# Output rows of a mixture-of-experts kernel: plain stores in token order in place of indexed writes

## The chip, the cores and the metric

The kernel runs on one core of one Trainium2 chip. The metric is the device time of one execution in microseconds (us), the median over runs. TensorE (PE), VectorE (DVE), ScalarE (ACT), GpSimd (POOL) and SyncE (SP) are separate engines; each works through its own queue of instructions in the order in which they were written, and semaphores hold an instruction until what it needs is done. SP computes nothing: here it starts most of the transfers between memory and the on-chip buffers. POOL also starts transfers, those that take their row numbers from a table.

## The reference

Eight sequences, each with 512 tokens of width 512 and 32 state tokens. An attention step lets tokens read from the states and states read from the tokens; the 544 rows that result, per sequence, go through a mixture of eight experts with one expert per row:

```python
xread = softmax(x @ state.T / 8) @ state          # 512 rows a sequence
sread = softmax(state @ x.T / 8) @ x              # 32 rows a sequence
for b in range(B):
    prev_e = -1
    for s in range(S):                            # S = 544
        fresh_e = argmax(logits[b, s])
        e = fresh_e if s == 0 or local_gate[b, s] < 0.5 or prev_e < 0 else prev_e
        prev_e = e
        p = softmax(logits[b, s])
        out[b, s] = p[e] * (relu(x[b, s] @ w1[e]) @ w2[e])
```

A row may keep the expert of the row before it. With the data of this case all 512 tokens of a sequence end up with the expert of its first token; the kernel does not rely on that, it counts what is left over.

## The kernel before

**The work.** A *unit* is the 512 tokens of one sequence, done with the expert of its first token (`slots.units`). There are eight units. The two matrix products of a unit (512 x 512 x 1024 and 512 x 1024 x 512) use a seven-product scheme in place of eight block products: sums of blocks of weights and inputs are made first on DVE (`first_sum`, `second_sum`, `column_sum`), then `seven` runs products 1, 5, 6, 2, 7, 3, 4 on PE, and ACT and DVE combine the results. A unit has two first halves (`first_half(0)`, `first_half(1)`) and two second halves (`second_half(n)`), 28 products in all, some 1.73 us each. The state tokens of all sequences are sorted by expert into nine *tiles* of 32 rows by 4 quarter rows (`Tile`), which are placed between the halves of units 4 to 7. A general path (`rows_again`, `more`) under `tc.If(left > 0)` does the tokens whose expert isn't that of their unit. Here none are left, so every engine reads `left` (L1244), jumps over that code (L1246) and meets the others in the closing steps (L1281).

**The order.** It is written out by hand. After each product `seven` calls `tick()`, and work that belongs beside the products is registered by tick number: attention of sequences 2 to 7 (`FLOW`, 14 ticks a sequence), the sums, and the steps of the routing (`GROUPS`, seven ticks for each group of sequences, the steps of the generator `choose`). Steps registered for the same tick are issued in the order in which they were registered, attention ahead of routing. The second step of `choose` is one ACT instruction, `activation(pr, pr, Act.Exp)` at L582. It needs `pr`, which the first step makes with its last DVE instruction (L579). For the first group of sequences these two steps are at ticks 6 and 7; tick 7 is the last of `first_half(0)` of unit 0, so that the exponent stands on ACT just ahead of the copy of product 1 of `first_half(1)` into `sum` (L995, `nc.scalar.copy(y, x)`). Product 6 adds to `sum`, so PE needs that copy.

**The output.** `second_half(n)` makes two blocks of 128 rows: `y0`, complete after product 3 (L1113), and `y1`, complete after product 4 (L1117 or L1119). Each is written with an indirect transfer from POOL (`scatter`, L1038): the row numbers are in `slots.tok`, made by one DVE instruction in `choose` (L615) from a table of token numbers (`self.token`, two POOL instructions in `more_constants`) and with 8192 added for a token that is not done here, so that the bounds check drops its row. The write of `y0` is issued at once; that of `y1` goes into the list `behind` and is issued during the next half. A tile's result is put into the same list and is written, also indirectly, by `Tile.scatter` (L985). The write of a unit's rows is declared free of dependencies only where `apart` is set, that is in the last `second_half` of the last unit (`scatter(..., not late)`). The others, and all writes of tiles, may touch any row of `out` as far as the framework can tell, so each waits until the one before it has landed. In that last half (`seven(..., apart=True)`) the list `waiting` holds the `y1` of the half before and the result of the last tile: the first is issued after product 6, the second after product 7.

**SP's queue.** SP starts the loads of weights (`load`, L842), of the units' inputs (`load_x`, L845), of the tiles' weights (L952, L954), of the attention's inputs (L292, L296), and the attention's stores (L463, L418). A load into a buffer waits on SP until the buffer's last reader is done, and everything behind it on SP waits too. Each of these transfers also waits until the one eight places earlier on SP has landed, since they share eight semaphores in turn. `load(u + 1, 1)`, the second weights of the next unit, comes right after the last `second_half` of unit `u`.

Of the kernel before, what the change touches and what calls it, by code (L numbers as in the profile page):

```python
# [18 lines left out]
P = 128  # L19
# [3 lines left out]
T = S + N  # L23
# [93 lines left out]
class Slots:  # L117


    def __init__(self, pool):  # L120

        self.tok = pool.tile([P, B, SC], I32, name="tok")
        self.prob = pool.tile([P, B, NC], F32, name="prob")
        self.state = pool.tile([P, NTILE], I32, name="state")
        self.row = pool.tile([P, NTILE], I32, name="row")
        self.probq = pool.tile([P, NTILE], F32, name="probq")
        self.rest_tok = pool.tile([P, NB], I32, name="rest_tok")
        self.rest_row = pool.tile([P, NB * Q], I32, name="rest_row")
        self.rest_prob = pool.tile([P, NB], F32, name="rest_prob")
        self.first = pool.tile([1, 1], I32, name="first")  # L130
        self.units = pool.tile([1, B], I32, name="units")
        self.tiles = pool.tile([1, NTILE], I32, name="tiles")
        self.rest = pool.tile([1, NREST], I32, name="rest")
        self.left = pool.tile([1, 1], I32, name="left")
        self.number = pool.tile([1, 1], I32, name="number")
# [23 lines left out]
"""  # L159
FIRST, PERIOD = 2, 14  # L160
PER = 28
GROUPS = {(0, 2): (6, 7, 10, 11, 13, 14, 15), (2, 4): (55, 56, 57, 59, 61, 62, 63),
          (4, 8): (102, 103, 105, 106, 109, 110, 111)}
ONES = 18, 19, 21, 22, 24, 25, 27, 28, 29

# [304 lines left out]
class Routing:  # L470
# [16 lines left out]
    def more_constants(self):  # L487
        nc, rt = self.nc, self.rt
        pi = rt.tile([P, 1], I32, name="pi")
        nc.gpsimd.iota(pi, pattern=[[0, 1]], base=0, channel_multiplier=1)  # L490
        ti, ci, bi = [rt.tile([P, B, NC], I32, name=n) for n in ("ti", "ci", "bi")]
        nc.gpsimd.iota(ti, pattern=[[T, B], [P, NC]], base=0, channel_multiplier=1)
        nc.gpsimd.iota(ci, pattern=[[-T // LOW, B], [-P // LOW, NC]], base=NT // LOW, channel_multiplier=0)
        nc.gpsimd.iota(bi, pattern=[[-1, B], [0, NC]], base=B, channel_multiplier=0)
        self.iob = rt.tile([P, P], BF16, name="iob")
        nc.gpsimd.tensor_copy(self.iob, self.io)
        self.identb = rt.tile([P, P], BF16, name="identb")
        nc.gpsimd.tensor_copy(self.identb, self.ident)
        self.part = rt.tile([P, 1], F32, name="part")
        nc.gpsimd.tensor_copy(self.part, pi)  # L500
        self.token = rt.tile([P, B, NC], F32, name="token")
        nc.gpsimd.tensor_copy(self.token, ti)
        self.ones = rt.tile([P, P], BF16, name="ones")
        nc.gpsimd.memset(self.ones, 1.0)
        self.one = rt.tile([1, P], F32, name="one")
        nc.gpsimd.memset(self.one, 1.0)
        self.on = rt.tile([P, E, COLS + 1], F32, name="on")
        nc.gpsimd.memset(self.on, 1.0)
        nc.gpsimd.memset(self.on[:, :, 0:1], 0.0)
        self.ons = rt.tile([SQ, E, B + 1], F32, name="ons")  # L510
        nc.gpsimd.memset(self.ons, 1.0)
        nc.gpsimd.memset(self.ons[:, :, 0:1], 0.0)
        self.turn = rt.tile([P, Q, SQ], BF16, name="turn")
        nc.gpsimd.tensor_copy(self.turn, self.iob[:, :SQ].rearrange("p (o t) -> p o t", o=1).to_broadcast([P, Q, SQ]))
        self.ex = rt.tile([P, B, NC], F32, name="ex")
        nc.gpsimd.memset(self.ex, 0.0)
        self.undone = rt.tile([P, B, NC], F32, name="undone")
        nc.gpsimd.memset(self.undone, 0.0)
        self.factors = rt.tile([P, B, NC, 6], BF16, name="factors")
        nc.gpsimd.tensor_copy(self.factors[:, :, :, 0], ci)  # L520
        nc.gpsimd.tensor_copy(self.factors[:, :, :, 5], bi)
        self.ev = rt.tile([P, E, 1], F32, name="ev")
        nc.vector.tensor_scalar(self.ev.rearrange("p e o -> p (e o)"), self.iof[:, :E], 1.0, None, Alu.add)
        self.before = rt.tile([P, P], BF16, name="before")
        nc.vector.tensor_scalar(self.before, self.iob, self.part, None, Alu.is_gt)
        nc.vector.tensor_scalar(self.factors[:, :, :, 1], self.ex, self.part, None, Alu.add)
        quarter = rt.tile([P, 1], I32, name="quarter_of")
        nc.vector.tensor_scalar(quarter, pi, SQ.bit_length() - 1, None, Alu.logical_shift_right)
        self.quarter = rt.tile([P, 1], F32, name="quarter")
        nc.vector.tensor_scalar(self.quarter, quarter, float(Q * NT), None, Alu.add)  # L530
        self.squarter = rt.tile([P, 1], F32, name="squarter")
        nc.vector.tensor_scalar(self.squarter, quarter, float(Q * B * N), None, Alu.add)
        self.mx = rt.tile([P, B, NC, 1], F32, name="mx")
        self.eq = rt.tile([P, B, NC, E], F32, name="eq")
        self.own = rt.tile([P, B, NC], F32, name="own")
        self.top = rt.tile([P, B, NC], BF16, name="top")
        self.pr = rt.tile([P, B, NC, E], F32, name="pr")
        self.zp = rt.tile([P, B, NC], F32, name="zp")
        self.oh = rt.tile([P, E, B, NC], BF16, name="oh")
        self.hold = rt.tile([B, T], BF16, name="hold")  # L540
        self.ran = rt.tile([B, T], BF16, name="ran")
        self.states = rt.tile([SQ, E, B], BF16, name="states")
# [13 lines left out]
    def choose(self, bank, b0, b1):  # L556
# [45 lines left out]
        for i in range(SC):  # L602
# [9 lines left out]
        nc.vector.scalar_tensor_tensor(self.undone[:, b, :SC], ex[:, b, :SC], -1.0,  # L612
                                       held.rearrange("p (b o) -> p b o", o=1).to_broadcast([P, n, SC]),
                                       Alu.add, Alu.not_equal)
        nc.vector.scalar_tensor_tensor(slots.tok[:, b], self.undone[:, b, :SC], float(OFF), self.token[:, b, :SC],  # L615
                                       Alu.mult, Alu.add)
        yield

        oh = self.oh[:, :, b].rearrange("p e b i -> p e (b i)")
# [188 lines left out]
class Experts:  # L808
# [84 lines left out]
    def run(self, start):  # L893
# [38 lines left out]
        class Tile:  # L932
# [49 lines left out]

            def scatter(self, y):
                at = bass.IndirectOffsetOnAxis(ap=slots.row[:, self.i:self.i + 1], axis=0)
                nc.gpsimd.indirect_dma_start(out=out.rearrange("n (q x) -> (n q) x", q=Q), out_offset=at, in_=y,  # L985
                                             in_offset=None, bounds_check=NT * Q - 1, oob_is_err=False)

        def seven(y, n, product, copies, whole, tick, waiting=(), apart=False):

# [9 lines left out]
            tick()  # L999
            product(y, 6)  # L1000
            two(y)
            for results in waiting[:1]:
                results()
            tick()
            product(x, 2)
# [2 lines left out]
            if apart:  # L1008
# [2 lines left out]
                tick()  # L1011
                product(y, 7)
                three(y)
                for results in waiting[1:]:
                    results()
                whole(4, None)
                tick()
                z = bank()[:, :n]
# [14 lines left out]
            whole(3, y)  # L1033
            tick()

        def scatter(at, y, apart=False):
            to = bass.IndirectOffsetOnAxis(ap=at, axis=0)
            put = nc.gpsimd.indirect_dma_start(out=out, out_offset=to, in_=y, in_offset=None, bounds_check=NT - 1,  # L1038
                                               oob_is_err=False)
            if apart:  # L1040
                tc.declare_no_dep(put.ins, group="scatters", reason="a token has one slot, so scatters write other rows")
                tc.add_to_no_dep_group("scatters", put.ins)

        def first_product(to, i, n, begin=False):

# [39 lines left out]
            seven(sums, 512, lambda to, i, begin=False: first_product(to, i, n, begin),  # L1085
                  [kept(flat(t)) for t in (s5, s2, s7)], whole, tick, waiting)

        def second_half(at, prob, n, tick, waiting, behind, late):
            ((d11, d12), (d21, d22)), wcs = places(1)
            seconds = {1: (h11, d11), 2: (h21, d21), 3: (hs[2], d22), 4: (h22, wcs[2]), 5: (hs[0], wcs[0]),  # L1090
                       6: (hs[1], wcs[1]), 7: (c12, d12)}
            r5, r2, r7 = [h1.tile([P, 2, UNIT // 2], F32, name=f"s{i}")[:, 0] for i in range(3)]
            at = [at[:, 2 * b + n:2 * b + n + 1] for b in range(2)]
            p0, p1 = [prob[:, 2 * b + n:2 * b + n + 1] for b in range(2)]
            y0, y1 = ys[2 * n:2 * n + 2]
            low, high = slice(0, D // 2), slice(D // 2, D)
# [10 lines left out]
            def second_whole(i, t):  # L1107
# [3 lines left out]
                    add(y1[:, high], r7, r5)  # L1111
                elif i == 2:
                    nc.vector.scalar_tensor_tensor(y0[:, high], t, p0, r2, Alu.mult, Alu.add)  # L1113
                    scatter(at[0], y0, not late)
                else:
                    if late:
                        scaled(y1[:, low], p1)(t)  # L1117
                    else:
                        nc.vector.scalar_tensor_tensor(y1[:, low], t, p1, r7, Alu.mult, Alu.add)  # L1119
                    behind.append(lambda: scatter(at[1], y1, not late))  # L1120

            seven(sums, D // 2, second, [scaled(r5, p1), scaled(r2, p0), scaled(r7, p1)], second_whole,
                  tick, waiting, apart=not late)
# [20 lines left out]
        def unit(u, waiting=()):  # L1144
# [9 lines left out]
                self.load_x(u + 1)  # L1154
                load(u + 1, 0)
            behind = []
            second_half(slots.tok[:, u], slots.prob[:, u], 0, self.tick, waiting, behind, True)
            bound(U * u + 2, behind)
            if not ahead:
                nc.gpsimd.drain()  # L1160
            waiting, behind = behind, []
            second_half(slots.tok[:, u], slots.prob[:, u], 1, self.tick, waiting, behind, ahead)
            bound(U * u + 3, behind)
            if not ahead:
                for results in behind:
# [51 lines left out]
        def more(v):  # L1217
# [15 lines left out]
                first_half(n, nothing)  # L1233
            for n in range(2):
                behind = []
                second_half(slots.rest_tok[:, U * v:U * v + U], slots.rest_prob[:, U * v:U * v + U], n, nothing, (),
                            behind, False)
                for results in behind:
                    results()
            if v + 1 < NREST:  # L1240
# [44 lines left out]
```

## Time and profile before

| what | value |
|---|---|
| median of 3 runs | 512.46 us (511.43, 512.46, 514.82) |
| the profiled execution's own time | 511.91 us |
| its span, first to last instruction | 510.1 us |
[...]
| busy, PE / DVE / ACT / POOL | 97% / 55% / 32% / 22% |
| DMA, mean rate | 227 GB/s |

The span is 1.8 us shorter than the execution's time; the rest lies around it. The median of the runs is 0.55 us above the profiled execution. An engine's busy share says how much of the span it had an instruction in work, whatever stage that was; the waits and the timeline say where an engine stood still and for whom.

### The profile page before, as it was taken

The numbers are of one execution on the slowest core, as the hardware profiler recorded it, in microseconds if no ns is written. First come the engines' busy times: TensorE is split into PE (matmuls) and PEld (weight loads), VectorE is DVE, ScalarE is ACT, GpSimd is POOL, SyncE is SP. The second block draws the span as 40 slices with busy tenths as digits, with TensorE's granted clock in tenths as the row PEclk, the third lists the DMA queues.
The fourth block names the chain that finished last, engine by engine and source line by source line (L and its number), as shares of the span: only waits on it lengthen the run. The fifth ranks groups of instructions, "written<-read, shape, count | busy, mean of one in ns | idle before, by whom it ended". The sixth has DMA issues, their size and how long they took to land. (4 is left out here: it accounts for less than half of the span.)

```text
span 510.1 us, 10091 instructions
## 1 busy us (share of the span) xinstructions
PE 494.8 (97%) x4008; PEld 390.4 (77%) x4008; DVE 282.0 (55%) x543; ACT 161.0 (32%) x334; POOL 111.6 (22%) x134
## 2 busy tenths in 40 slices
PE   8899999999999999999999999999999999999992
PEld 2457787776877778787888888888888888878881
DVE  5878885497765986436576745155342624346100
ACT  2625424353343443434223322223122321223210
POOL 6602232322232223220021202210101300121012
PEclk9999999999999999999999999999999999999997
DMA  8995472917649074441746976793989579593411
GB/s 306 348 331 185 163 278 108 358 35 258 243 135 340 26 261 159 141 175 55 275 129 223 400 249 213 246 410 128 397 330 350 202 279 410 194 340 125 169 41 53
DMA packets 38289, 115.67 MB, mean 227 GB/s; under 512 B 7749, under 2 KB 7881, under 8 KB 34009
## 3 DMA queue, kind: packets, MB, share of 16 engines
q1 hardware_dynamic: 34952, 105.37, 57.0%
q0 software_dynamic: 3136, 9.51, 4.9%
q8 instruction: 33, 0.54, 0.4%
q14 instruction: 24, 0.19, 0.1%
q10 hardware_dynamic: 144, 0.07, 0.0%
HBM read 97.10 MB, written 17.89 MB: 225 GB/s over the span
## 5 line engine op out<-in xcount | busy, mean ns | idle before, releaser
L1054 PE MATMUL ps<-x,a 128*128 128x256 f32 x384 | 92.8, 384 | 0.0
L1054 PE MATMUL sum<-xs,a 128*128 128x256 f32 x384 | 91.6, 381 | 1.2 <-ACT sum L995 1.2
L1038 POOL DMA_INDIRECT out_dram<-y,tok x32 | 37.2, 1163 | 236.3 <-DVE xs L852 47.8
L1054 PEld LDWEIGHTS sum<-xs,a 128*128 128x128 f32 x384 | 71.9, 190 | 15.9 <-issue 2.5
L1054 PEld LDWEIGHTS ps<-x,a 128*128 128x128 f32 x384 | 71.3, 190 | 14.5 <-issue 5.2
L1101 PE MATMUL ps<-c,h 128*128 128x256 f32 x264 | 63.8, 385 | 0.0
L1101 PE MATMUL ps<-c,hs 128*128 128x256 f32 x256 | 60.8, 380 | 0.0
L1101 PE MATMUL sum<-c,h 128*128 128x256 f32 x248 | 58.7, 379 | 0.0
L1101 PEld LDWEIGHTS ps<-c,h 128*128 128x128 f32 x264 | 49.0, 190 | 9.5 <-issue 2.9
L1101 PEld LDWEIGHTS ps<-c,hs 128*128 128x128 f32 x256 | 48.4, 190 | 9.0 <-issue 2.5
L1101 PEld LDWEIGHTS sum<-c,h 128*128 128x128 f32 x248 | 46.6, 190 | 6.1
L852 DVE TENSOR_TENSOR a<-a,a 128x1024 f32<-128x1024 f32 x32 | 40.2, 1294 | 4.5 <-DMA a<-in_w_dram 4.3
L852 DVE TENSOR_TENSOR c<-c,c 128x1024 f32<-128x1024 f32 x32 | 39.9, 1280 | 2.8 <-DMA c<-in_w_dram 2.5
L852 DVE TENSOR_TENSOR h<-s,s 128x512 f32<-128x512 f32 x16 | 11.1, 696 | 43.2 <-ACT s L1083 43.1
L995 ACT COPY sum<-ps 128x512 f32<-128x512 f32 (+1 forms) x32 | 14.8, 464 | 55.4 <-PE ps L1101 27.9
L1054 PE MATMUL ps<-xs,a 128*128 128x256 f32 x128 | 30.7, 382 | 0.5 <-DVE a L852 0.5
L1083 ACT COPY s<-sum 128x512 f32<-128x512 f32 x32 | 18.7, 585 | 38.5 <-PE sum L1054 30.3
L1101 PE MATMUL sum<-c,hs 128*128 128x256 f32 x128 | 30.9, 384 | 0.0
L1101 PEld LDWEIGHTS sum<-c,hs 128*128 128x128 f32 x128 | 23.8, 190 | 8.0 <-issue 2.5
L1105 ACT ACTIVATE s<-sum,prob 128x256 f32<-128x256 f32 x32 | 15.1, 473 | 46.1 <-PE sum L1101 44.9
L852 DVE TENSOR_TENSOR y<-s,s 128x256 f32<-128x256 f32 x16 | 6.8, 424 | 39.0 <-ACT s L1105 39.0
L1054 PEld LDWEIGHTS ps<-xs,a 128*128 128x128 f32 x128 | 24.0, 190 | 4.7 <-DVE a L852 1.4
(186 smaller groups left out, 562.9 us busy)
## 6 DMA issues: line engine op xcount, KB each, us to landing
at<-in_w_dram SPq DMA_DIRECT2D x18, 1024.0 KB, 7.4
ct<-in_w_dram SPq DMA_DIRECT2D x18, 1024.0 KB, 10.2
a<-in_w_dram SPq DMA_DIRECT2D x32, 512.0 KB, 7.8
c<-in_w_dram SPq DMA_DIRECT2D x32, 512.0 KB, 6.5
x_t<-in_xt_dram SPq DMA_DIRECT2D x16, 512.0 KB, 6.1
x_n<-in_xn_dram SPq DMA_DIRECT2D x8, 1024.0 KB, 6.9
xts<-xr SPq DMA_DIRECT2D x28, 256.0 KB, 2.1
x<-xts SPq DMA_DIRECT2D x7, 1024.0 KB, 5.8
```

The lines of the kernel that those rows point to most:

```text
L852: self.nc.vector.tensor_tensor(out, a, b, op=op)
L995: nc.scalar.copy(y, x)
L1038: put = nc.gpsimd.indirect_dma_start(out=out, out_offset=to, in_=y, in_offset=None, bounds_check=NT - 1, oob_is_err=False)
L1054: nc.tensor.matmul(to[:, m * width:m * width + width], lhsT=w[:, j, f:f + P], rhs=x[:, j, :], start=begin and m == 0 and j == 0, stop=(m = ...
L1083: return lambda t: nc.scalar.copy(to, t)
L1101: nc.tensor.matmul(to, lhsT=x[:, m, n * P:n * P + P], rhs=w[:, m, :], start=begin and m == 0, stop=(m == FK // 2 - 1), skip_group_check=True)
L1105: return lambda t: nc.scalar.activation(to, t, Act.Copy, scale=p)
```

## The change

- The rows of a unit are written by `unit_rows`, a plain store issued on SP, 128 consecutive rows of `out` each, at the same places in the order in which `scatter` stood. All rows are written, also those of tokens of another expert; the general path writes over them afterwards (`rest_rows`, the indirect write as before, ordered behind everything).
- The stores of units and the writes of tiles are declared to touch different rows, each towards the group of the other (`apart`). The writes of tiles stay in order among themselves.
- `slots.tok`, the table `token` and the instructions that make them are gone: two POOL instructions at the start, one DVE instruction in each of the three groups of `choose`.
- In the last half of the last unit everything in `waiting`, the last tile's write too, is issued after product 6.
- In the first group of sequences the exponent of `choose` moves from tick 7 to tick 9.

```diff
-GROUPS = {(0, 2): (6, 7, 10, 11, 13, 14, 15), (2, 4): (55, 56, 57, 59, 61, 62, 63),
+GROUPS = {(0, 2): (6, 9, 10, 11, 13, 14, 15), (2, 4): (55, 56, 57, 59, 61, 62, 63),
...
-        nc.gpsimd.iota(ti, pattern=[[T, B], [P, NC]], base=0, channel_multiplier=1)
...
-        self.token = rt.tile([P, B, NC], F32, name="token")
-        nc.gpsimd.tensor_copy(self.token, ti)
...
-        nc.vector.scalar_tensor_tensor(slots.tok[:, b], self.undone[:, b, :SC], float(OFF), self.token[:, b, :SC],
-                                       Alu.mult, Alu.add)
...
             def scatter(self, y):
...
+                put = nc.gpsimd.indirect_dma_start(out=out.rearrange("n (q x) -> (n q) x", q=Q), out_offset=at, in_=y,
+                                                   in_offset=None, bounds_check=NT * Q - 1, oob_is_err=False)
+                apart(put, "states", "x")
...
-            for results in waiting[:1]:
+            for results in waiting if apart else waiting[:1]:
                 results()
...
                 three(y)
-                for results in waiting[1:]:
-                    results()
...
+        def apart(put, rows, others):
+
+            tc.declare_no_dep(put.ins, group=others, reason="x tokens and state tokens have rows of their own")
+            tc.add_to_no_dep_group(rows, put.ins)
+
+        def unit_rows(u, c, y):
+            apart(nc.sync.dma_start(out=out[u * T + c * P:u * T + c * P + P], in_=y), "x", "states")
+
+        def rest_rows(v, c, y):
+            to = bass.IndirectOffsetOnAxis(ap=slots.rest_tok[:, U * v + c:U * v + c + 1], axis=0)
+            nc.gpsimd.indirect_dma_start(out=out, out_offset=to, in_=y, in_offset=None, bounds_check=NT - 1,
+                                         oob_is_err=False)
...
                     nc.vector.scalar_tensor_tensor(y0[:, high], t, p0, r2, Alu.mult, Alu.add)
-                    scatter(at[0], y0, not late)
+                    put(v, n, y0)
...
-                    behind.append(lambda: scatter(at[1], y1, not late))
+                    behind.append(lambda: put(v, 2 + n, y1))
...
-            second_half(slots.tok[:, u], slots.prob[:, u], 0, self.tick, waiting, behind, True)
+            second_half(unit_rows, u, slots.prob[:, u], 0, self.tick, waiting, behind, True)
...
-            second_half(slots.tok[:, u], slots.prob[:, u], 1, self.tick, waiting, behind, ahead)
+            second_half(unit_rows, u, slots.prob[:, u], 1, self.tick, waiting, behind, ahead)
```

## Rows read from the trace of the kernel before

**Rows 1.** Part 1 of the page: busy time, share of the span, instructions
```profile
PE 494.8 (97%) x4008; PEld 390.4 (77%) x4008; DVE 282.0 (55%) x543; ACT 161.0 (32%) x334; POOL 111.6 (22%) x134
```

**Rows 2.** PE's waits, first and last of eight: us in total, times, longest
```profile
PE sum L1054 <- ACT sum L995: 1.2, 1, 1.2
...
PE s L320 <- DMA x_t<-in_xt_dram: 0.2, 1, 0.2
```

**Rows 3.** Timeline of PE, 33 to 62 us: start us, us, engine, line, instruction, idle before
```profile
44.96 1.89 PE L1054 MATMUL ps<-xs,a 128*128 128x256 f32 x8
48.09 1.99 PE L1054 MATMUL sum<-xs,a 128*128 128x256 f32 x8 [1.24 <-ACT sum L995]
...
59.10 1.89 PE L1101 MATMUL ps<-c,h 128*128 128x256 f32 x8
60.83 1.46 PE L1101 MATMUL ps<-c,hs 128*128 128x256 f32 x6
```

**Rows 4.** Timeline of ACT, 40 to 66 us
```profile
47.28 0.27 ACT L582 ACTIVATE pr<-pr 128x80 f32<-128x80 f32 x1 [3.25 <-DVE pr L579]
47.45 0.58 ACT L995 COPY sum<-ps 128x512 f32<-128x512 f32 x1
```

**Rows 5.** Timeline of DVE, 33 to 62 us
```profile
47.01 0.23 DVE L579 TENSOR_TENSOR pr<-lt,mx 128x80 f32<-128x80 f32 x1
...
55.24 0.77 DVE L852 TENSOR_TENSOR h<-s,s 128x512 f32<-128x512 f32 x1 [0.36 <-ACT s L1083]
```

**Rows 6.** Timeline of all engines, 478 to 512 us
```profile
487.71 0.35 DVE L980 TENSOR_SCALAR yt<-ps,probq 128x128 f32<-128x128 f32 x1 [3.16 <-PE ps L976]
...
497.85 0.98 POOL L1038 DMA_INDIRECT out_dram<-y,tok  x1 [5.86 <-DVE y L1113]
...
499.97 0.48 DVE L1119 SCALAR_TENSOR_TENSOR y<-ps,prob,s 128x256 f32<-128x256 f32 x1 [0.80 <-PE ps L1101]
501.21 0.98 POOL L985 DMA_INDIRECT out_dram<-yt,row  x1 [2.39 <-DMA out_dram<-y,tok]
504.53 0.98 POOL L1038 DMA_INDIRECT out_dram<-y,tok  x1 [2.35 <-issue]
```

**Rows 7.** Line L1244, by engine: instruction, count, ns min/median/max, first and last start
```profile
L1244 SPq TENSOR_LOAD <-left x1: 275/275/275, 472.2 to 472.2; - x1
```

**Rows 8.** Line L1246, the jump over the general path, SP and ACT
```profile
L1246 SPq EVENT_SEMAPHORE  x9: 17/17/17, 478.2 to 478.8; - x9
...
L1246 ACTq EVENT_SEMAPHORE  x2: 17/17/17, 502.0 to 502.1; - x2
...
L1246 SPq COMPARE_BRANCH  x1: 45/45/45, 472.5 to 472.5; - x1
...
L1246 ACTq COMPARE_BRANCH  x1: 50/50/50, 498.8 to 498.8; - x1
```

**Rows 9.** Line L1281, the closing steps on SP
```profile
L1281 SPq EVENT_SEMAPHORE  x14: 17/28/28, 508.5 to 510.1; - x14
```

**Rows 10.** Line L463, stores of 256 KB from SP; us from issue to landing
```profile
L463 SPq DMA_DIRECT2D xts<-xr x28: 319/320/794, 34.0 to 241.5; - x28
...
DMA to landing us min/median/max: 2.0/2.9/6.9
```

**Rows 11.** Timeline of SP, 250 to 300 us: second weights of unit 4
```profile
258.63 9.76 SPq L842 DMA_DIRECT2D c<-in_w_dram  x4
```

**Rows 12.** Line L842 from 255 us on, loads of weights: us from issue to landing
```profile
DMA to landing us min/median/max: 5.0/9.0/14.0
```

**Rows 13.** Timeline of DVE, 263 to 291 us
```profile
268.06 0.48 DVE L1113 SCALAR_TENSOR_TENSOR y<-ps,prob,s 128x256 f32<-128x256 f32 x1 [0.80 <-PE ps L1101]
...
283.84 3.62 DVE L852 TENSOR_TENSOR c<-c,c 128x1024 f32<-128x1024 f32 x3
```

**Rows 14.** Timeline of PE, 264 to 300 us
```profile
296.36 1.89 PE L1101 MATMUL ps<-c,hs 128*128 128x256 f32 x8
```

**Rows 15.** Timeline of POOL, 0 to 75 us
```profile
10.12 2.05 POOL L357 TENSOR_TENSOR e<-e,m 128x512 f32<-128x512 f32 x2 [3.86 <-DVE m L350]
```

More of the change, by code (lines that the diff above doesn't have):

```diff
@@ L120, in __init__ @@
     def __init__(self, pool):
-        self.tok = pool.tile([P, B, SC], I32, name="tok")
         self.prob = pool.tile([P, B, NC], F32, name="prob")
@@ L490, in more_constants @@
         nc.gpsimd.iota(pi, pattern=[[0, 1]], base=0, channel_multiplier=1)
-        ti, ci, bi = [rt.tile([P, B, NC], I32, name=n) for n in ("ti", "ci", "bi")]
-        nc.gpsimd.iota(ti, pattern=[[T, B], [P, NC]], base=0, channel_multiplier=1)
+        ci, bi = [rt.tile([P, B, NC], I32, name=n) for n in ("ci", "bi")]
         nc.gpsimd.iota(ci, pattern=[[-T // LOW, B], [-P // LOW, NC]], base=NT // LOW, channel_multiplier=0)
@@ L984, in scatter @@
                 at = bass.IndirectOffsetOnAxis(ap=slots.row[:, self.i:self.i + 1], axis=0)
-                nc.gpsimd.indirect_dma_start(out=out.rearrange("n (q x) -> (n q) x", q=Q), out_offset=at, in_=y,
-                                             in_offset=None, bounds_check=NT * Q - 1, oob_is_err=False)
+                put = nc.gpsimd.indirect_dma_start(out=out.rearrange("n (q x) -> (n q) x", q=Q), out_offset=at, in_=y,
+                                                   in_offset=None, bounds_check=NT * Q - 1, oob_is_err=False)
+                apart(put, "states", "x")
         def seven(y, n, product, copies, whole, tick, waiting=(), apart=False):
@@ L1034, in seven @@
             tick()
[L1036 to L1042, printed above, removed]
+        def apart(put, rows, others):
[7 more added lines that the diff above has]
+                                         oob_is_err=False)
         def first_product(to, i, n, begin=False):
@@ L1086, in first_half, with second_half @@
                   [kept(flat(t)) for t in (s5, s2, s7)], whole, tick, waiting)
-        def second_half(at, prob, n, tick, waiting, behind, late):
+        def second_half(put, v, prob, n, tick, waiting, behind, late):
             ((d11, d12), (d21, d22)), wcs = places(1)
@@ L1092, in second_half @@
             r5, r2, r7 = [h1.tile([P, 2, UNIT // 2], F32, name=f"s{i}")[:, 0] for i in range(3)]
-            at = [at[:, 2 * b + n:2 * b + n + 1] for b in range(2)]
             p0, p1 = [prob[:, 2 * b + n:2 * b + n + 1] for b in range(2)]
@@ L1235, in more @@
                 behind = []
-                second_half(slots.rest_tok[:, U * v:U * v + U], slots.rest_prob[:, U * v:U * v + U], n, nothing, (),
-                            behind, False)
+                second_half(rest_rows, v, slots.rest_prob[:, U * v:U * v + U], n, nothing, (), behind, False)
                 for results in behind:
```

## The prediction

> **What bounds the kernel now.** I read the busy shares first. PE has an instruction in work for 494.8 us of a span of 510.1 [rows 1], so anything that only frees POOL, DVE or the transfer queues is worth nothing; a gain must come from the 15 us in which PE has nothing, or from PE work, and the change removes none of that. Next I read what PE itself waited for. The list has eight lines; the longest single wait is 1.2 us, for ACT's copy into `sum` [rows 2]. All of it lies in the attention stage and unit 0. Then the end: the last result `y1` is finished by DVE at 499.97 + 0.48 = 500.45, and the span ends at 510.1 [rows 6, 9]. So 9.65 us pass after the last arithmetic. These two places, one stall at 48 us and the end, decide this change; the rest of it needs a check for harm only.
>
> **The early stall.** Product 5 starts at 44.96 and product 6 at 48.09 [rows 3], 3.13 us apart, where neighbours without a wait are 60.83 - 59.10 = 1.73 us apart. The loss is 1.40 us (the 1.24 in the row counts from the modelled end of the matmul before). Its cause stands on ACT: the exponent of `choose` sat idle there for 3.25 us, until DVE had `pr` at 47.01 + 0.23 = 47.24, and only behind it came the copy of product 1 into `sum`, at 47.45 [rows 4, 5]. PE's product 6 was waiting for just that copy. With the exponent at tick 9 the copy goes out as soon as product 1 is done, before product 5 ends, and product 6 starts at 44.96 + 1.73 = 46.69.
>
> What is late next? At its new place the exponent stands ahead of ACT's copy of product 6, which can't start before 46.69 + 1.73 = 48.42; `pr` is there at 47.24 and the exponent takes 0.27 [rows 4], so it fits into the 1.2 us between. DVE is nearer to the limit. Its sum `h` at 55.24 had been idle for 0.36 us only [rows 5]: of the 1.40 us, 1.04 can't be followed there. PE needs what comes of it in product 5 of the second half, at 60.83 [rows 3], in future at 59.43. The sum would run at 54.88; counting four steps on DVE and ACT (itself and three more) of 0.77 each, an estimate from its own row, gives 57.96. That leaves 1.5 us, so PE takes the whole 1.40. The bounds are 0 (another wait fills the hole) and 1.40; I take 1.40, since the nearest later need has room. From there to the end no wait of PE's is listed, so the shift is carried to the last product.
>
> **The end.** Before: the last three writes go through POOL one at a time. `y0` is issued at 497.85; the tile's write at 501.21 had waited for that one's landing (2.39 us idle); the last `y1` is issued at 504.53, 3.32 us after the tile's [rows 6], although its data was ready at 500.45. Then POOL jumps over the general path, SP sees its last semaphore at 508.5 and the closing steps run to 510.1 [rows 9].
>
> After: the last tile's result is ready at 487.71 + 0.35 = 488.06 [rows 6]. Its write is now issued after product 6 and waits for no unit's rows, so it is off the path by more than 10 us, and POOL's jump with it. The chain that is left runs on SP, from DVE's last result on:
> - the store's issue, 0.32 us [rows 10];
> - the read of `left`, 0.28 us [rows 7];
> - the jump. ACT's took 502.0 - 498.8 = 3.2 us from the branch to the next instruction; SP's own, while weights were still loading, 478.2 - 472.5 = 5.7 us [rows 8]. I take 3.2, as SP will now jump with one store in flight, and keep 5.7 as the far end;
> - nine semaphore steps, 478.8 - 478.2 = 0.6 us [rows 8];
> - the closing steps, 510.1 - 508.5 = 1.6 us [rows 9];
> - 0.2 us for the gaps between these, an estimate from the starts in the rows on SP.
>
> The sum is 6.2 us against 9.65: a gain of 3.45 us (with 5.7 for the jump, 0.95). The store itself lands 2.0 to 2.9 us after its issue as a rule, 6.9 at most among loads [rows 10]; the jump starts 0.6 us after the issue and takes 3.2, so the landing is covered. A landing of 6.9 would end the span at 500.45 + 6.9 + 1.6 = 508.95 before the shift by 1.40, a gain of 1.15.
>
> **What is costed at nothing, and its cover.** POOL loses 32 descriptor issues and two constants. In the head POOL stood idle 3.86 us for DVE right behind the constants [rows 15], so these two gain nothing. The three DVE instructions for `tok` are in DVE's queue, on which PE doesn't wait. Without that cover they would be worth about half a microsecond, three times the 0.2 us or so of such a small step (an estimate from `pr`'s 0.23 in rows 5).
>
> SP gets 32 stores, four a unit, 0.32 us each, some 10 us of issue time spread over the run. What matters is what they hold back, since a store waits on SP for its data. `y1` is stored a half later and is long finished. `y0` is stored at the product that makes it. Behind the second `y0` of a unit stand the four loads of the next unit's second weights. In unit 3 these went out from 258.63 to 258.63 + 9.76 = 268.39, as their buffers came free [rows 11]; `y0` is finished at 268.06 + 0.48 = 268.54 [rows 13], so the first is held for 9.9 us and the fourth for hardly any. Four issues of 0.32 later, at 269.9, all are out. The slowest landing of such a load takes 14.0 us, the median 9.0 [rows 12]: 279 to 284. DVE took up their sums at 283.84 for 3.6 us and more [rows 13]; PE wants the first of them at 296.36 [rows 14]. That is 8.7 us of room at the worst end, so the cost is zero. The bytes are those of before; each store puts 256 KB ahead of loads in SP's own queue.
>
> **The sum.** 1.40 + 3.45 = 4.85 us. The profiled execution took 511.91 us for a span of 510.1; it becomes 507.06. The median of the runs is 0.55 us above that execution, so I forecast 512.46 - 4.85 = 507.6 us, 0.95% faster. About 1%, here 5.1 us, is what a measurement can tell from no change; the bound is at 507.3, and the forecast sits on it.
>
> **The rivals.**
> 1. *The end shortens little* (0.15). SP's jump takes its 5.7 us again, or the store lands late. The row for it is the only jump that SP made; against it, loads filled the queues then. Gain 0.95 + 1.40: 510.1 us. A neighbouring reading (0.03 of the 0.15): only the issue gets cheaper, 0.98 us on POOL against 0.32 on SP [rows 6, 10], so 0.66 + 1.40 and 510.4. The two waits at 501.21 and 504.53 speak against it. [...] The trace shows a second thing at stake, the order among the writes.
> 2. *The early stall comes back* (0.10), through DVE at 55 us or an ACT copy behind the moved exponent: 512.46 - 3.45 = 509.0 us.
> 3. *SP's jump is free* (0.08), its 45 ns and no more [rows 8], because the target is already there. Then the landing of the last store, 2.9 us [rows 10], sets the end: 2.9 + 1.6 + 0.1 against 9.65 gives 5.05, with 1.40 a time of 506.0 us. Every jump in the rows speaks against it. [...]
> 4. *Slower: SP is held and weights come late* (0.05). The mechanism is the held loads above, at the seven boundaries between units. It decides from the point where the weights land more than 8.7 us later than I reckoned, which takes the 14.0 us landing to nearly 23. For a loss of over 1% PE would have to stand 5.1 + 4.85 = 10 us, 1.4 at each boundary; with 2 us at each the time is 507.6 + 14 = 521.6 us. For it speaks that in unit 3 the loads did run ahead; against it that the room is there.
>
> The forecast has the remaining 0.62.
>
> **How the numbers follow.** The forecast's own range is 506.6 to 508.6: the jump within 0.3 us, and 0.7 for the spread of a median of runs whose two lower values lie 1.0 apart. The bound at 507.3 cuts it, 0.30 faster and 0.32 the same. With rival 3 faster gets 0.38; rivals 1 and 2 add 0.25 to the same, 0.57; slower is 0.05. The range from 505.9 to 510.4 takes in rivals 1 to 3 and leaves out the fourth and a little of the spread.
>
> **What would show it.** In the trace after: product 6 of `first_half(1)` in unit 0 starts 1.73 us after product 5, and PE's list has no wait for ACT's `sum` there; the last matmul ends 1.4 us earlier; no POOL write after about 490; the last store starts within 0.1 us of DVE's last result; from that result to the end 6.2 us, most of it between SP's branch and its next instruction. I am wrong if that stretch is near 9, if PE shows new waits between 50 and 62 us, or if PE waits for sums of `a` or `c` at the start of a half.

## The result and the profile after

The changed kernel took 507.57 us, the median of six runs (507.05 to 508.85), against 512.84 us for the kernel before (six runs, 511.43 to 514.82): a ratio of 0.990, 95% interval 0.987 to 0.993. The forecast was 507.6. The profiled execution took 507.64 us for a span of 505.8; the one before had 511.91 and 510.1, so the two traces differ by 4.3 us.

**PE is still the bound.** Part 1 of the page of the changed kernel, beside [rows 1]:

```profile
PE 494.1 (98%) x4006; PEld 390.4 (77%) x4008; DVE 280.0 (55%) x540; ACT 161.4 (32%) x334; POOL 73.0 (14%) x100
```

POOL lost 38.6 us of work and 34 instructions, DVE its three for `tok`. PE's busy time is that of before within 0.7 us, so the gain lies where PE had nothing to do.

**The early stall.** PE's waits (engine, what it waited for: us in total, times, longest), first and last of six, beside [rows 2]:

```profile
PE p L282 <- DVE warm L218: 1.2, 1, 1.2
...
PE p L447 <- ACT x L456: 0.3, 1, 0.3
```

ACT's copy into `sum` has gone from the list. The timelines of PE, ACT and DVE there (start us, us, engine, line, instruction, idle before), beside [rows 3], [rows 4] and [rows 5]:

```profile
44.73 1.89 PE L1052 MATMUL ps<-xs,a 128*128 128x256 f32 x8
46.46 1.89 PE L1052 MATMUL sum<-xs,a 128*128 128x256 f32 x8
...
57.37 1.89 PE L1098 MATMUL ps<-c,h 128*128 128x256 f32 x8
59.10 1.24 PE L1098 MATMUL ps<-c,hs 128*128 128x256 f32 x5
```

```profile
44.99 0.57 ACT L990 COPY sum<-ps 128x512 f32<-128x512 f32 x1 [1.18 <-PE ps L1052]
...
47.82 0.27 ACT L578 ACTIVATE pr<-pr 128x80 f32<-128x80 f32 x1
```

```profile
46.79 0.23 DVE L575 TENSOR_TENSOR pr<-lt,mx 128x80 f32<-128x80 f32 x1
...
54.58 1.22 DVE L846 TENSOR_TENSOR h<-s,s 128x512 f32<-128x512 f32 x1
```

Products 5 and 6 start 1.73 us apart where 3.13 passed before. The copy now runs at 44.99, the exponent at 47.82, 2.8 us behind it. DVE's sum `h` has no idle time left ahead of it, and PE's first products of the second half follow each other without a wait.

**The end.** The timeline of all engines from 485 us on, SP's rows too, beside [rows 6]:

```profile
485.98 0.35 DVE L974 TENSOR_SCALAR yt<-ps,probq 128x128 f32<-128x128 f32 x1 [3.15 <-PE ps L970]
486.61 0.98 POOL L979 DMA_INDIRECT out_dram<-yt,row  x1 [14.91 <-DVE yt L974]
...
495.40 3.69 SPq L1035 DMA_DIRECT2D out_dram<-y  x2
...
498.24 0.48 DVE L1116 SCALAR_TENSOR_TENSOR y<-ps,prob,s 128x256 f32<-128x256 f32 x1 [0.79 <-PE ps L1098]
```

The tile's write is out at 486.61, 0.3 us behind its data; before it went at 501.21. DVE ends `y1` at 498.72 and the second of SP's two stores ends its issue at 495.40 + 3.69 = 499.09. What follows on SP, three lines of the code (read of `left`, jump, closing steps; ns min/median/max, first and last start), beside [rows 7], [rows 8] and [rows 9]:

```profile
L1240 SPq TENSOR_LOAD <-left x1: 273/273/273, 499.1 to 499.1; - x1
```

```profile
L1242 SPq EVENT_SEMAPHORE  x9: 17/17/17, 503.1 to 503.7; - x9
...
L1242 DVEq EVENT_SEMAPHORE  x2: 21/21/21, 503.1 to 503.2; - x2
...
L1242 DVEq COMPARE_BRANCH  x1: 72/72/72, 498.9 to 498.9; - x1
L1242 SPq COMPARE_BRANCH  x1: 45/45/45, 499.5 to 499.5; - x1
```

```profile
L1277 SPq EVENT_SEMAPHORE  x14: 17/28/28, 503.7 to 505.8; - x14
```

From DVE's last result to the end 505.8 - 498.7 = 7.1 us pass, where it was 9.65 us and 6.2 were forecast: store and read 0.7, SP's jump 503.1 - 499.5 = 3.6, nine steps 0.6, closing 2.1.

The 4.3 us between the two traces are 1.40 at the stall, 9.65 - 7.1 = 2.55 at the end, and some 0.3 that the changed kernel was already ahead by at 44.73 (44.96 before) and won in small pieces up to 60 us.

**The held loads.** The timeline of SP around the start of unit 4, beside [rows 11], then the landing of these loads, beside [rows 12], DVE's sums and PE's first use, beside [rows 13] and [rows 14]:

```profile
253.38 13.83 SPq L1035 DMA_DIRECT2D out_dram<-y  x3
267.79 2.10 SPq L836 DMA_DIRECT2D c<-in_w_dram  x4
```

```profile
DMA to landing us min/median/max: 7.2/10.7/13.8
```

```profile
282.11 3.61 DVE L846 TENSOR_TENSOR c<-c,c 128x1024 f32<-128x1024 f32 x3
```

```profile
294.63 1.89 PE L1098 MATMUL ps<-c,hs 128*128 128x256 f32 x8
```

The four loads leave from 267.79, where they had left from 258.63 on: held by the store of `y0`, as foreseen. In the trace the last of them has landed at 277.4; DVE took up the sums at 282.11, 1.73 us earlier than before, in step with PE, and had no idle time ahead of them. PE's list has no wait behind 62 us, so none at the other boundaries either. On DVE the waits for weights are no longer than before (2.5 to 1.3 us in all for `c`, 4.3 to 4.0 for `a`); those for the units' inputs, which SP loads too, grew from 25.7 to 28.3 us, at no cost to PE.

### The profile page after: what moved, and what is told of

The parts are those of the page before. It is cut to its first block, busy times and chain, and to the rows that moved or that the text cites. A ratio compares the mean times of both kernels' runs of the same rounds, so it can differ in the third digit from the quotient of the medians.

```text
span 505.8 us, 10013 instructions
## 1 busy us (share of the span) xinstructions
PE 494.1 (98%) x4006; PEld 390.4 (77%) x4008; DVE 280.0 (55%) x540; ACT 161.4 (32%) x334; POOL 73.0 (14%) x100
## 4 chain that ended last, share of the span: by engine, by line
PE 95%; DMA 1%; DVE 1%; POOL 1%; SPq 0%; issue 0%; DVEq 0%; POOLq 0%
PE ps L1098 23%; PE ps L1052 22%; PE sum L1052 17%; PE sum L1098 16%; PE ps L970 3%; PE ps L957 3%; PE p L447 3%; PE s L319 2%; DMA a<-in_w_dram 1%; PE p L402 1%; PE p L389 1%; PE p L282 1%; PE p L434 1%; PE p L422 0%; POOL e L379 0%; DVE e L346 0%
## 5 line engine op out<-in xcount | busy, mean ns | idle before, releaser
L922 POOL DMA_INDIRECT xgt<-rows,state x9 | 10.1, 1124 | 140.9 <-DVE probq L714 72.6
```

What stands on the lines that cost most here:

```text
L922: nc.gpsimd.indirect_dma_start(out=to.rearrange("p k x -> p (k x)"), out_offset=None, in_=rows.rearrange("n q x -> (n q) x"), in_offset=ba ...
```

## The experiments

Two questions were open: whether the gain splits into the stall and the end as forecast, and what at the end brings it: **theory**, the order among the writes, so that nothing waits for another write's landing; **rival**, the issue on SP in place of POOL. The times below are medians of four to twelve runs. They come in three sets; the kernels of one set ran on one chip, beside the kernel before.

### The first set: the parts one by one

The kernel before had 512.26 us here (17 runs). The changed kernel once more:

> The changed kernel once more, as the measure for the others on the same chip. Theory (two places: the early stall of PE, and the order among the last writes): 507.6 us, 5.2 below the kernel before, a ratio of 0.990; span near 505.8, first_half(1) of unit 0 without a wait for ACT's copy. Any theory expects the same; the spread between this and the first timing says how small a difference the others can show.

**Measured:** 506.93 us, ratio 0.990 (0.988 to 0.991).

The changed kernel with the exponent at its old tick:

```diff
-GROUPS = {(0, 2): (6, 9, 10, 11, 13, 14, 15), ...
+GROUPS = {(0, 2): (6, 7, 10, 11, 13, 14, 15), ...
```

> The changed kernel with the exponent of the first group back at tick 7; everything else as changed. Theory: PE's stall of 1.4 us between products 5 and 6 of first_half(1) of unit 0 is back and is carried to the end, 509.0 us (1.4 above the changed kernel), last matmul 1.4 later. Rival (the stall was hidden, all of the gain comes from the writes): 507.6, as the changed kernel, with the stall made good before the end of unit 0.

**Measured:** 508.98 us, ratio 0.994 (0.992 to 0.996). The stall is back where it was. Timeline of PE of this kernel:

```profile
44.81 1.89 PE L1052 MATMUL ps<-xs,a 128*128 128x256 f32 x8
47.95 1.99 PE L1052 MATMUL sum<-xs,a 128*128 128x256 f32 x8 [1.24 <-ACT sum L990]
```

3.14 us apart: 1.41 lost at the place. The medians lie 2.05 us apart, the fastest runs of the two 1.78 (508.20 and 506.42, both at a mean granted TensorE clock of 0.998 of full speed).

The kernel before with the exponent moved, and nothing else (the same line, 7 to 9):

> The kernel before with the exponent of the first group at tick 9 and nothing else of the change. Theory: 1.4 us below the kernel before, 511.4 us, a ratio of 0.997; the end after the last DVE result stays at 9.6 us. Rival (the writes alone count): the time of the kernel before.

**Measured:** 510.71 us, ratio 0.997 (0.996 to 0.999): 1.55 us by the medians. Its end is the old one, 9.9 us from DVE's last result; POOL's writes in its timeline:

```profile
496.71 0.98 POOL L1038 DMA_INDIRECT out_dram<-y,tok  x1 [5.86 <-DVE y L1113]
500.03 0.98 POOL L985 DMA_INDIRECT out_dram<-yt,row  x1 [2.34 <-DMA out_dram<-y,tok]
503.60 0.98 POOL L1038 DMA_INDIRECT out_dram<-y,tok  x1 [2.60 <-DVEq L1246]
```

The three writes still go out 3.3 and 3.6 us apart.

The kernel before with the exponent moved, its indirect writes kept on POOL, all of them declared to touch different rows, and the last tile's write after product 6 (`free` is true outside the general path):

```diff
+                tc.declare_no_dep(put.ins, group="scatters", reason="x tokens and state tokens have rows of their own")
+                tc.add_to_no_dep_group("scatters", put.ins)
...
-            for results in waiting[:1]:
+            for results in waiting if apart else waiting[:1]:
...
-                    scatter(at[0], y0, not late)
+                    scatter(at[0], y0, free)
...
-                    behind.append(lambda: scatter(at[1], y1, not late))
+                    behind.append(lambda: scatter(at[1], y1, free))
```

> The kernel before with the exponent at tick 9, all indexed writes of units and tiles declared free of each other, and the last tile's write issued after product 6; the writes stay indexed and on POOL, slots.tok stays. Theory (the order among the writes is what cost at the end): the last write is issued within 0.3 us of DVE's last result, POOL's jump (2.9 us) runs beside its landing (3.1), so 6 to 7 us from that result to the end and 507.2 us (506.7 to 508), level with the changed kernel. Rival (the gain comes from the move to SP, plain stores in place of indexed ones): no gain beyond that of the exponent, 511.4 us.

**Measured:** 506.75 us, ratio 0.990 (0.988 to 0.993), the time of the changed kernel. POOL's timeline of this kernel, last rows, and DVE's last result:

```profile
489.00 0.98 POOL L1038 DMA_INDIRECT out_dram<-y,tok  x1 [4.70 <-ACT sum L997]
490.29 0.98 POOL L985 DMA_INDIRECT out_dram<-yt,row  x1 [0.31 <-issue]
495.83 0.98 POOL L1038 DMA_INDIRECT out_dram<-y,tok  x1 [4.57 <-issue]
498.73 0.98 POOL L1038 DMA_INDIRECT out_dram<-y,tok  x1 [1.92 <-DVE y L1119]
...
497.97 0.48 DVE L1119 SCALAR_TENSOR_TENSOR y<-ps,prob,s 128x256 f32<-128x256 f32 x1 [0.80 <-PE ps L1101]
```

The tile's write follows the unit's after 1.3 us, not 3.3, and the last `y1` leaves 0.3 us after DVE's result at 498.45; from there to the end 6.2 us pass. The rival falls: with the order gone, the issuing engine makes no difference that these runs can show. Plain stores, the table of indices and the move to SP are not what pays.

### The second set: what is left of the end

The kernel before had 511.59 us here (7 runs). The changed kernel without its declarations, so that the stores of units and the writes of tiles wait for each other (the stores of units, each with rows of its own that stand in the program, still don't wait for one another: no declaration covers them in the changed kernel either, and there the store issued at 484.57 left while that of 482.90 was in flight until 484.93):

```diff
         def apart(put, rows, others):
+            return
```

> The changed kernel without the declarations: stores of units and writes of tiles wait for each other's landing again where the framework can't tell their rows apart. Theory: the last tile's write is issued after product 6 and long landed when the last stores come, and SP has room for a wait of some 4 us at a y0 store in units 5 to 7, so the time is that of the changed kernel, 507 us (within 0.7), with the same 6.6 to 7.1 us from DVE's last result to the end. Rival (the declared independence itself is what is gained): 2 us or more above the changed kernel, 509 or more.

**Measured:** 507.04 us, ratio 0.991 (0.989 to 0.992), the time of the changed kernel. The order is really back; SP's waits (us in total, times, longest) have a line for it:

```profile
SPq L1036 <- DMA out_dram<-yt,row: 35.3, 4, 13.9
```

But it costs nothing once the tile's write is issued early: in this profile that goes at 487.92 and has landed by 490.5, the `y0` on SP goes at 495.94 and the last `y1` at 499.28, 0.03 us after its data. From `y1` to the end 6.3 us pass, a little less than the 6.6 expected. The run on POOL kept the old engine and the indirect writes, this one kept the order; each is as fast as the changed kernel. What both have and the kernel with the moved exponent alone lacks is the last tile's write ahead of the last two products instead of between them. No run made this step alone, with writes both on POOL and ordered, so that it would be enough by itself is argued, not shown.

The last `y1` stored from ACT, so that SP can jump early:

```diff
-            apart(nc.sync.dma_start(out=out[u * T + c * P:u * T + c * P + P], in_=y), "x", "states")
+            engine = nc.scalar if (u, c) == (B - 1, 3) else nc.sync
+            apart(engine.dma_start(out=out[u * T + c * P:u * T + c * P + P], in_=y), "x", "states")
```

> The changed kernel with the very last store, y1 of the last half, issued from ACT in place of SP, so that SP jumps earlier and its nine semaphore steps are off the path. Theory (the engine that issues the last store must read left and jump after it, and that jump is the largest part of the end): the end shrinks by those nine steps, 0.6 us, to 6.0 to 6.4 us, and the time to 506.4 us. Rival (the landing of the last store sets the end): no change.

**Measured:** 506.32 us, ratio 0.989 (0.988 to 0.991), 0.7 us under the kernel without declarations, the nearest one in this set, with intervals that overlap. The line of the jump in this kernel (as above):

```profile
L1243 SPq EVENT_SEMAPHORE  x9: 17/17/17, 499.1 to 502.6; - x9
...
L1243 ACTq EVENT_SEMAPHORE  x2: 17/17/17, 503.1 to 503.2; - x2
L1243 SPq COMPARE_BRANCH  x1: 45/45/45, 496.4 to 496.4; - x1
...
L1243 ACTq COMPARE_BRANCH  x1: 54/54/54, 500.0 to 500.0; - x1
```

SP's 2.6 us jump is now off the path; ACT's, 3.1 us, takes its place, but SP's nine steps run beside it. Eight of them are done at 499.6. The ninth stands at 502.6, where in the trace the last part of ACT's store lands, 3.5 us after its issue. So the rival was close: ACT's jump ends only 0.5 us behind that landing. From `y1` to the end 5.9 us pass.

The changed kernel without the general path. It leaves out the code for tokens whose expert isn't that of their unit (there are none in the data), with the read of `left` and the jump:

> The changed kernel without the general path: the read of left, the jump and the code behind it are left out, so tokens of other experts would not be done over (with this data there are none). Theory: no engine jumps after the last result; the end is the store's issue (0.33), its landing (2.0 to 2.9) and the closing steps (1.6 to 2.1), 4.0 to 5.3 us in place of 6.6 to 7.1, and the time 505.0 us. Rival (the landing sets the end, the jump runs beside it): the end stays within 0.3 us.

**Measured:** 504.32 us, ratio 0.986 (0.984 to 0.987), 2.7 us under the run with the declarations off. DVE's last row of this kernel:

```profile
498.71 0.48 DVE L1116 SCALAR_TENSOR_TENSOR y<-ps,prob,s 128x256 f32<-128x256 f32 x1 [0.80 <-PE ps L1098]
```

From `y1` (499.20) to the end of the span (502.6) 3.4 us pass, where the changed kernel has 6.5 to 7.1 us and the one without declarations 6.3. That is shorter than the 4.0 to 5.3 us expected.

Not all of this is the jump. The stores land sooner too. From issue to landing, the `y0` of the last half, first in the changed kernel, then without the general path:

```profile
DMA to landing us min/median/max: 3.3/3.3/3.3
```

```profile
DMA to landing us min/median/max: 2.0/2.0/2.0
```

By the trace the last `y1` takes 3.6 us to land in the changed kernel (2.8 and 2.6 in its two later profiles), most of its 16 parts 1.8 to 2.0 us and the last two longer; without the general path all 16 are in after 2.0. So the changed kernel's last store had landed at 502.3, only 0.7 us before SP came out of its jump at 503.1. So the general path goes with two delays: the jump, and a later landing that the jump just covers. Why the landing is later was not tested; the packets below are in flight at the same time.

What fills a jump? The transfers of the last stretch by queue (packets, MB, share of the 16 engines' time), first of the changed kernel from 498.7 us on, then of the one without the general path from 499 us on:

```profile
q14 instruction: 5, 0.04, 1.4%
q8 instruction: 1, 0.02, 0.9%
```

```profile
q14 instruction: 1, 0.01, 0.9%
```

In the run with the jump six packets move in the queues that the profile calls `instruction`, in the one without it one. That part of a jump is a wait for code to come in is my reading of this label; no run tested it. SP's jump takes 2.6 to 3.6 us in the profiles in which no weights are loading then (2.6 with the last store on ACT; 3.6, 3.1 and 2.9 in the changed kernel). The packets don't fill all of it: from 501.1 to 503.0, with SP and DVE still in their jump, the only packets that move in the changed kernel are the store's (queue, packets, MB, share):

```profile
q1 hardware_dynamic: 7, 0.01, 1.9%
```

What the engines wait for in these last 2 us is open.

### The third set: the spread, and a better version

The kernel before had 512.18 us here (11 runs). In some executions the changed kernel loses time in the attention stage: in the profile from the first set PE's first product of unit 0 starts at 27.26 where the trace of the result has 25.14, and DVE's last result comes 1.7 us later (500.40 against 498.72). Three runs side by side: the changed kernel again; the same with seven more dummy matmuls (`kp`) where PE stood idle between 15 and 24 us; and both these dummies and the last store on ACT.

> The changed kernel once more, as the base of the two runs beside it. Theory A (the spread of 1 to 2 us between executions comes from a stretch between 20 and 30 us in which TensorE's granted clock sits at half, 3.4 or 6.8 us long, in some executions and not in others): the slower executions show a lower mean clock, 0.991 to 0.995, the faster ones 0.996 to 0.998, and the median is 506.8 to 507.6 us. Theory B (the spread lies elsewhere, in the end of the span or in the transfers): time and clock don't go together.

```diff
-... tb01 kp2 sr0 ... kp1 lg0 ... fe0 vv00 ... tb10 kp2 sr1 ...
+... tb01 kp3 sr0 ... kp4 lg0 ... fe0 kp1 vv00 ... tb10 kp4 sr1 ...
```

> The changed kernel with seven more dummy matmuls in the attention stage at the places where PE stood idle between 15 and 24 us (0.27 to 0.65 us each), in four steps of the written order. Theory A: PE then has work through these gaps, the half-clock stretch is rarer or gone, the executions lie closer together (within 0.8 us) and the median falls by 0.3 to 0.8 us against the base beside it. Theory B: the spread stays as it is and the median is the base's, or up to 0.8 us above it, where the dummies stand in the way of real products (7 x 0.21 = 1.5 us of matmuls, about half of it into idle time).

> The same seven dummy matmuls, and the last store of the last unit issued on ACT, as in the run with that change alone. The two effects lie at opposite ends of the kernel, so they should add: 0.7 us from the store (506.32 against 507.04 beside it) and whatever the dummies alone give, 505.7 to 506.4 us. If the 0.7 us of the store was spread between runs, the time is that of the run with the dummies alone.

**Measured:** 507.73, 507.42 and 505.85 us; ratios 0.9925 (0.9908 to 0.9942), 0.991 (0.990 to 0.993) and 0.988 (0.986 to 0.989). The first is 0.1 us above the range expected. Busy time of each engine from 20 to 30 us (then TensorE's granted clock as a share of full speed, DMA share, GB/s): the changed kernel in the first set, then in this one, then the one with the dummies:

```profile
20.00:30.00 10.00, 9.63 (x121) 6.20 (x122) 6.29 (x16) 3.24 (x8) 2.05 (x2) 0.66 0.84 279
```

```profile
20.00:30.00 10.00, 9.01 (x136) 5.72 (x136) 6.19 (x16) 3.67 (x9) 2.05 (x2) 0.83 0.85 288
```

```profile
20.00:30.00 10.00, 9.38 (x141) 5.32 (x143) 6.05 (x15) 3.59 (x9) 2.05 (x2) 1.00 0.88 306
```

Time and clock go together in the main, as the first theory has it: of six executions of the changed kernel the fastest had a mean clock of 0.997, the two slowest 0.991 (509.06 and 509.19 us). The clock isn't all of it: of the runs on POOL two had 0.995, and took 507.03 and 508.55 us. The cure failed: with the dummies five runs still spread from 506.71 (0.998) to 508.35 (0.993), where 0.8 us was expected, and the profile of the third kernel has 0.83 in this stretch again. Whether they help is unclear; the intervals overlap.

The third kernel is the fastest full one: 1.9 us under the changed kernel beside it, with intervals that don't meet. It lies in the range expected from adding the two effects. But the store on ACT alone gave 0.7, within the spread; how the rest divides between the dummies and the clock of four runs stays open.

## Why the prediction was right, point by point

- **PE bounds, and the gain is in the stall and the end.** Right: 1.40 and 2.55 of the 4.3 us between the traces lie there.
- **The early stall, 1.40 us.** Right at the place, 1.40 in the trace of the result and 1.41 when it was put back. By whole runs the move is worth a little more, 1.55 on the kernel before and 2.05 on the changed one; the second difference contains more low-clock runs on the side with the stall (three of six at 0.992 or less, against one of six). DVE's idle time ahead of `h` was used up, as worked out, and DVE held nothing up.
- **The end, 9.65 to 6.2 us.** The mechanism was right, the size too good: 7.1, 6.6 and 6.5 us in three profiles of the changed kernel. One term was too small in all three: the closing steps took 2.1 us, not 1.6. The jump was 3.6, 3.1 and 2.9 against 3.2. It covered the landing, as foreseen, with 0.7 to 1.0 us to spare, though the last store took 2.6 to 3.6 us to land, where 2.0 to 2.9 was taken as the rule. I took ACT's jump as the price; that SP would jump while DVE was still in its own (498.9 to 503.1) was not considered, and both came out at the same moment.
- **The gain comes from the order among the writes.** Right, and narrower than written: with the tile's write issued after product 6, the plain stores could be left out, and so could the declarations. Both at once were not left out in any run.
- **POOL's issues, the constants and `tok` cost and give nothing.** Right: POOL's 38.6 us less left no trace in the time, since the version that keeps them is as fast.
- **SP's held loads cost nothing.** Right, but the working has one step too few. I counted 8.7 us up to PE's product at 296.36. DVE takes up the sums of `c` in the order of its queue, at 283.84 before, and the slowest landing was reckoned at 284: for that load the room up to DVE was nothing. A wait there would have moved DVE's work first, and PE's only once the 8.7 us were used up. In the run the loads were all out at 269.89, later than reckoned (269.9, less the 1.7 us by which everything had moved up), yet the slowest had landed at 277.4, 4.7 us before DVE took the sums up.
- **The total.** 4.85 us forecast, 5.27 by the medians of the first six runs, 5.33 and 4.45 against the kernel before in the first and third set, 4.3 between the two traces. The end gave 0.25 to 0.9 us less than reckoned, the stall and the head a little more. That 507.57 meets the forecast of 507.6 so closely is luck: the kernel before came out 0.4 us slower in six runs than in the three that I started from, the gain 0.4 us larger, and the two cancel.
- **The rivals.** The end did shorten, the stall did not come back, no load came late. The jump was not free: the branch itself took 45 ns on SP and 72 on DVE, but 2.9 to 3.6 us passed on SP before the next instruction. The run without it gains 7.3 us on the kernel before beside it, where a free jump was to give 6.45: its end took 3.4 us where I had reckoned 4.6, with 2.9 for the landing of the last store; its stores landed in 2.0.

## What to carry to other kernels

Look at the last writes of a kernel in their order of issue: two that may touch the same rows wait for each other's landing, some 3.3 us each here, and it can be enough to issue the one whose data is early before the last products. A branch over code that is never run isn't free when it stands behind the last result: leaving out the general path gave 2.7 us here by the medians, jump and landing together, while the choice of engine and kind of store gave nothing that shows. An instruction that waits in an in-order queue, ahead of one that PE needs, can hold PE up: here 1.40 us of the 3.25 that it waited. The rows of PE and of the instruction behind it show what it costs and where it may stand.

## What the hardware showed that was not expected

- **Two jumps at once ended together.** In three profiles of the changed kernel DVE branches about 0.6 us ahead of SP and both go on within 0.15 us of each other; DVE's jump took 4.2, 3.8 and 3.7 us there, 2.9 in the kernel before, where SP had jumped long ago. Whether one holds the other up was not tested. Why it is 2.9 to 3.6 us on SP from one execution to the next is open.
- **TensorE's clock falls in a busy stretch, in some executions only.** In the attention stage its mean from 20 to 30 us was 0.83 or 0.66 of full speed in two profiles of the changed kernel, after PE had stood idle several times for 0.27 to 0.65 us. At half speed (the level granted at the end of the changed kernel, 0.50 from 502 to 505.8 us) that comes to 3.4 or 6.8 us, an estimate from these means. In the first profile of the changed kernel it stayed up (1.00 from 20 to 30 us), though PE stood idle there in the same places, 0.27 to 0.65 us. Against that profile DVE's last result came 0.6 us later with the mean of 0.83 and 1.7 us later with 0.66. Filling most of these gaps did not prevent it: the third kernel of the last set has 0.83 there.
- **The closing steps vary by kernel:** 1.6 us in the kernel before, in the one that writes on POOL and in the one without declarations; 2.1 in every profile of the changed kernel. The difference lies on POOL: from its clearing of the semaphores to its last drain 0.56 us pass in the changed kernel (504.86 to 505.42), 0.21 in the kernel before. What it waits for there was not found.
